# First-layer products of a maxout FFN as eleven block products instead of twelve, in the last two token groups

## The chip, the cores and the metric

The kernel runs on one core of one Trainium2 chip. The metric is the device time of one execution in microseconds (us), the median of several runs. Everything is float32.

## The reference

A DeltaNet attention (batch 4, 8 heads, 768 steps, head dimension 48) feeds a feed-forward block with a maximum of three linear layers (3072 tokens, width 384, hidden width 768):

```python
for t in range(S):
    kt, vt, bt = (k_n[:, :, t], v[:, :, t], beta[:, :, t, None])
    y[:, :, t] = np.einsum('bhd,bhde->bhe', q[:, :, t], state)
    v_old = np.einsum('bhde,bhd->bhe', state, kt)
    state = state + bt[:, :, :, None] * np.einsum('bhd,bhe->bhde', kt, vt - v_old)
...
h = np.maximum(np.maximum(x @ w1, x @ w2), x @ w3)
return (h @ w_out).astype(np.float32)
```

where `x` is `y` with the heads side by side: 3072 tokens of 384 numbers.

## The kernel before, in words

**Groups.** The sequence is cut into chunks of 64 steps. Two chunks of all four batches are a group of 512 tokens, and there are six groups, m = 0 to 5 (`GROUPS` = 6). For each group the kernel works out the recurrence (gram matrices, a triangular solve, state updates) and then the feed-forward block, `ffn(m)` (L1046). The two are interleaved: while TensorE does `ffn(m)`, the recurrence of group m+1 and the gram matrices and the solve of group m+2 are slipped in between its matmuls.

**Order.** The program is written in an order by hand (`manual_schedule`, L96): on every engine the instructions stand in the order in which the Python code issues them, and so do the DMAs on each queue. `ffn(m)` is a generator. The loop at L1320 takes it step by step; after step i it issues the small pieces that the table `LINKS` (L1210) names for i, then some columns of the solve (`some(solving, n)`, L1335). In the table a letter is a piece of work and a digit which chunk or unit it is for: k and q (the products of keys and queries with the state, L738, L747), z and j (two joining products of the triangular inverse, L694, L707), d (its turned copies on VectorE, L615), u (`new`, L753), s (state update, L771), y (L793), x, w and X (y goes to DRAM, comes back and is turned into the tokens `xt`, L833 to L866), g (gram matrices and their masks, L395), t (turned keys and queries, L375), and K, V, L, N (loads). Around the change the table is used with its last entries altered:

```python
LAST_LINKS = {**LINKS, 17: "", 19: "X1"}
```

**The first layer, `hidden` (L1050).** The second and third weights have had the first one subtracted (L868), and the first weight is multiplied into the output layer (L876 to L901), so from group 1 on a hidden tile is max(0, x·(w2−w1), x·(w3−w1)), and x·w1·w_out is added in the output layer. For each of six tiles of 128 hidden columns and each of the two weights, three matmuls (width 384 = 3 x 128) with 512 tokens moving fill one PSUM tile `p_h` (L1057), which ScalarE turns into `h` with a ReLU (L1067) or VectorE takes into the maximum (L1071). That makes twelve steps with 36 matmul instructions a group. `p_h` comes from `ps_ffn` (L80), two PSUM tiles of one bank in turn; the recurrence uses `ps_two` (L83), three tiles of two banks in turn.

**The output layer.** Groups 0 to 3 use plain matmuls (L1092). Groups 4 and 5 use `outputs` (L947), which already has seven products of 2x2 blocks in place of eight, with sums on VectorE (L989) and prepared weights `crossed` (`cross_weights`, L907, issued in `ffn(4)` at steps 8 and 9).

**The solve (L498).** For groups from 1 on, VectorE does 31 columns with two instructions each (L552, L556) on two tiles, `x_bl` and `y_bl`. `x_bl` comes from DRAM (L483), where the gram matrices `at` were put by 16 DMAs (L436). Ahead of the columns stand a square root on ScalarE (L261) and a dozen short VectorE instructions (L262 to L538). After the last column `y_bl` goes to DRAM (L577) and comes back as `ut` in eight DMAs (L586), which z needs. The solve of group 5 is done in `ffn(3)`; its last four `ut` loads are issued by `some(solving, 3)` after step 0 of `ffn(4)` (L1323).

Of the kernel before, what the change touches and what calls it, by code (L numbers as in the profile page):

```python
# [9 lines left out]
FP32 = mybir.dt.float32  # L10
# [4 lines left out]
ALU = mybir.AluOpType  # L15
# [3 lines left out]
BL = 32  # L19
HB = 16  # L20
# [3 lines left out]
def kernel(  # L24
# [31 lines left out]
    nc = tc.nc  # L56
# [5 lines left out]
    KT = DM // 128  # L62
    FT = DFF // 128
    NP = H // 2
    UNITS = NCH * 2
    GROUPS = UNITS // 4
    TOK = 512
# [4 lines left out]
    work = ctx.enter_context(tc.tile_pool(name="work", bufs=2))  # L72
# [7 lines left out]
    def ps_ffn(shape, name):  # L80
        return psum.tile(shape, FP32, name=name, tag="ffn", bufs=2)

    def ps_two(name):  # L83
        return psum.tile([128, 2, 512], FP32, name=name, tag="two", bufs=3)
# [3 lines left out]
    kmore = [const.tile([128, 2, H, DP], FP32, name=f"kmore{i}") for i in range(2)]  # L88
# [20 lines left out]
    def rows(bb):  # L109
        return slice(C * bb, C * (bb + 1))  # L110
# [25 lines left out]
    def load_v(c, queue=nc.sync):  # L136
        vts[c] = work.tile([128, 2, H, D], FP32, name="v_t", bufs=3)
        for bb in range(2):
            queue.dma_start(  # L139
                out=vts[c][rows(bb)].rearrange("p g h d -> p (g h) d"),  # L140
                in_=v[2 * bb : 2 * bb + 2, :, c * C : (c + 1) * C, :].rearrange(
                    "b h p d -> p (b h) d"
                ),
            )
# [36 lines left out]
    for bb in range(2):  # L181
        nc.gpsimd.affine_select(
            out=mask[rows(bb)], in_=mask[rows(bb)], pattern=[[1, C]], base=-1,
# [4 lines left out]
    t1 = [const.tile([128, 2, H, BL], FP32, name=f"t1{i}") for i in range(NU)]  # L188
# [5 lines left out]
    w_sb = [const.tile([128, KT, DFF], FP32, name=f"w{i}_sb") for i in range(3)]  # L194
# [112 lines left out]
    def square(name):  # L307
        return work.tile([128, H, C], FP32, name=name, tag="square", bufs=17)
# [39 lines left out]
    def load_blocks(n, queue=nc.gpsimd):  # L348
        c, g = divmod(n, 2)
        for i in range(2):  # L350
            if n % 4 == 2:
                t = kmore[i].rearrange("p a h d -> p (a h d)")[:, 0 : 2 * TURNED]
                t = t.rearrange("p (b x) -> p b x", b=2)
            else:
                t = work.tile(
                    [128, 2, TURNED], FP32, name="turned", tag="w_bits", bufs=5
                )
            turned[n, i] = t
            nc.gpsimd.memset(t[:, :, TURNED - 48 : TURNED], 0.0)  # L359
            for bb in range(2):  # L360
                for par in range(2):
                    for db in range(2):
                        p0, at = DP * par + 32 * db, 32 * (1 - db)
                        (queue, nc.gpsimd)[i].dma_start(  # L364
                            out=t[p0 : p0 + 32, bb, at : at + NP * 2 * D].rearrange(
                                "p (j x) -> p j x", j=NP
                            ),
                            in_=(k, q)[i][
                                2 * bb + g, :, c * C : (c + 1) * C, :
                            ].rearrange(  # L370
                                "(j two) (r tb) d -> two r j (tb d)", two=2, tb=2
                            )[par],
                        )
# [104 lines left out]
    def blocks(m, queue=nc.sync):  # L478
        if m == 1:
            xs[m] = in_wo(0)  # L480
        else:
            xs[m] = work.tile([128, 2, HB * BL + HB], FP32, name="x_bl", bufs=1)
        queue.dma_start(  # L483
            out=in_rows(xs[m]),
            in_=at_d[m].rearrange("c f b h j i -> (c f b h) j i"),
        )
# [232 lines left out]
    xts, rhss, qss, us, yts = {}, {}, {}, {}, {}  # L719
# [171 lines left out]
    def both_layers(t):  # L891
        p_m = ps_ffn([128, DM], "p_m")
        for f in range(FT):
            nc.tensor.matmul(  # L894
                p_m,
                w_sb[0][:, t, f * 128 : (f + 1) * 128],
                wo_sb[:, f],
                start=(f == 0),
                stop=(f == FT - 1),
            )  # L900
        nc.scalar.copy(w_sb[0][:, t, 0:DM], p_m)  # L901

    HALF = DM // 2
    PAIRS = FT // 2
    crossed = {}
# [41 lines left out]
    def outputs(m, hs):  # L947
# [95 lines left out]
        store(m5, 1, 1)  # L1043
        yield

    def ffn(m):  # L1046
        xt = xts[m]
        hs = {}

        def hidden(f, lo, w):  # L1050
            if f not in hs:
                hs[f] = square("h").rearrange("p h c -> p (h c)")
            h = hs[f][:, lo : lo + w]
            for i in range(m > 0, 3):
                p_h = ps_ffn([128, TOK], "p_h")[:, 0:w]
                for t in range(KT):
                    nc.tensor.matmul(  # L1057
                        p_h,
                        w_sb[i][:, t, f * 128 : (f + 1) * 128],
                        xt[:, t, lo : lo + w],  # L1060
                        start=(t == 0),
                        stop=(t == KT - 1),
                    )
                if i == 0:
                    nc.scalar.copy(h, p_h)
                elif m and i == 1:
                    nc.scalar.activation(  # L1067
                        out=h, in_=p_h, func=mybir.ActivationFunctionType.Relu
                    )
                else:  # L1070
                    nc.vector.tensor_tensor(out=h, in0=h, in1=p_h, op=ALU.max)  # L1071
                yield


        early = FT // 2 if m == 0 else 0
        for lo in (0, TOK // 2):
            for f in range(early):
                yield from hidden(f, lo, TOK // 2)
        for f in range(early, FT):
            yield from hidden(f, 0, TOK)  # L1080
        if m >= GROUPS - 2:
            yield from outputs(m, hs)
            return
        for i in range(4):
            cc, g = divmod(i, 2)
            p_o = ps_ffn([128, DM], "p_o")
            last = slice(i * 128, (i + 1) * 128)
            terms = [(hs[f][:, last], wo_sb[:, f]) for f in range(FT)]
            if m:
                terms += [(xt[:, t, last], w_sb[0][:, t, 0:DM]) for t in range(KT)]  # L1090
            for n, (stays, moves) in enumerate(terms):
                nc.tensor.matmul(  # L1092
                    p_o, stays, moves, start=(n == 0), stop=(n == len(terms) - 1)
                )
                if m and n == 4:
                    yield
            o_sb = work.tile([128, DM], FP32, name="o_sb")
            nc.scalar.copy(o_sb, p_o)  # L1098
            for bb in range(2):
                tok0 = (2 * bb + g) * S + (2 * m + cc) * C  # L1100
                nc.sync.dma_start(out=out[tok0 : tok0 + C, :], in_=o_sb[rows(bb)])
            yield
# [3 lines left out]
    def some(gen, n):  # L1106
        for _ in range(n):
            if next(gen, gen) is gen:
                break

    conv = weights()
    solving = solve(0)
# [71 lines left out]
    for _ in range(2):  # L1184
# [17 lines left out]
    solving = solve(1)  # L1202
# [33 lines left out]
        t=turn, K=load_k, L=lambda n: load_blocks(n, nc.sync),  # L1236
# [4 lines left out]
    def links(m, names):  # L1241
        for name in names.split():
            f, i = name[0], int(name[1])
            if f in RECURS and m < GROUPS:
                RECURS[f](2 * m + i)
            elif f in MADE and m + 1 < GROUPS:
                MADE[f](2 * (m + 1) + i)
            elif f in UNIT and m + 1 < GROUPS:
                UNIT[f](4 * (m + 1) + i)
            elif f == "N" and m + 2 < GROUPS:  # L1250
                load_blocks(4 * (m + 2) + i)
# [15 lines left out]
    for i, _ in enumerate(ffn(0)):  # L1267
# [17 lines left out]
        if i == 20:  # L1285
            solving = solve(2)
# [31 lines left out]
    UNIT.update(t=turn_blocks, K=lambda n: load_k(n, (nc.gpsimd, nc.gpsimd)))  # L1318
    MADE.update(V=lambda c: load_v(c, nc.gpsimd))
    for m in range(1, GROUPS):  # L1320
        for i, _ in enumerate(ffn(m)):
            if i == 0:
                some(solving, 3)  # L1323
            if m == 1 and i in (2, 5, 8):
                both_layers(i // 3)
            if m == GROUPS - 2 and i in (8, 9):
                cross_weights(i - 8)
            if m + 2 < GROUPS:
                if i == 6:
                    blocks(m + 2)  # L1330
                if i == 8:
                    solving = solve(m + 2)
            links(m + 1, (LAST_LINKS if m == GROUPS - 2 else LINKS).get(i, ""))
            if i > 7:
                some(solving, 3 if i > 8 else 1)  # L1335
# [29 lines left out]
```

## Time and profile before

| | |
|---|---|
| median of three runs | 514.99 us (511.83 to 518.12) |
| the profiled execution's own time | 514.26 us |
| its span, from the first to the last instruction | 512.3 us |
| VectorE, ScalarE, GpSimd busy | 324.2 us (63%), 163.7 us (32%), 192.3 us (38%) |
| `ffn(4)`, first layer, with recurrence pieces | 388.6 to 432.2 us |
| `ffn(4)`, output layer | 432.2 to 455.4 us |
| `ffn(5)`, first layer | 455.4 to 486.3 us |
| `ffn(5)`, output layer and stores | 486.3 to 512.3 us |

A line of the timeline reads: start in us, duration in us, engine, line of the code, operation, what is written and read, shape, count, and in brackets how long the engine had been idle and what ended that. PE is TensorE (PEld its weight loads), DVE VectorE, ACT ScalarE, POOL GpSimd, SPq the DMA queue of SyncE. A table of windows gives for each stretch its length, then the busy time and the number of instructions of each engine, the TensorE clock that was granted (1.00 is full speed), the share of DMA time and GB/s. A float32 matmul instruction appears as two records on PE, two passes: the first layer of group 5 has 36 instructions and 72 records.

### The profile page before, as it was taken

The numbers are of one execution on the slowest core, as the hardware profiler recorded it, in microseconds if no ns is written. First come the engines' busy times: TensorE is split into PE (matmuls) and PEld (weight loads), VectorE is DVE, ScalarE is ACT, GpSimd is POOL, SyncE is SP. The second block draws the span as 40 slices with busy tenths as digits, with TensorE's granted clock in tenths as the row PEclk, the third lists the DMA queues.
The fourth block names the chain that finished last, engine by engine and source line by source line (L and its number), as shares of the span: only waits on it lengthen the run. The fifth ranks groups of instructions, "written<-read, shape, count | busy, mean of one in ns | idle before, by whom it ended". The sixth has DMA issues, their size and how long they took to land.

```text
span 512.3 us, 18314 instructions
## 1 busy us (share of the span) xinstructions
PE 492.6 (96%) x7956; PEld 322.2 (63%) x7956; DVE 324.2 (63%) x735; ACT 163.7 (32%) x302; POOL 192.3 (38%) x317
## 2 busy tenths in 40 slices
PE   7778989999999999999999999999999999999996
PEld 6667778755565565665555565555655556974496
DVE  5897799868996430899553987635897244521142
ACT  5586664984422232200242101341101412101110
POOL 7444372783491925770575780503130000000000
PEclk9765999999999999999999999999999999999999
DMA  8938879874055926463775454823333202220002
GB/s 110 196 67 217 192 146 157 194 212 85 3 149 143 169 48 125 106 142 80 151 128 129 120 138 100 167 34 94 82 95 98 44 3 64 61 63 0 1 15 47
DMA packets 106303, 53.47 MB, mean 104 GB/s; under 512 B 89712, under 2 KB 99984, under 8 KB 106224
## 3 DMA queue, kind: packets, MB, share of 16 engines
q1 hardware_dynamic: 94640, 31.55, 30.9%
q0 software_dynamic: 9472, 20.37, 16.9%
q8 instruction: 62, 1.02, 0.9%
q10 hardware_dynamic: 2112, 0.39, 0.5%
q14 instruction: 17, 0.14, 0.1%
HBM read 39.17 MB, written 13.11 MB: 102 GB/s over the span
## 4 chain that ended last, share of the span: by engine, by line
PE 70%; DVE 15%; DMA 7%; issue 3%; ACT 2%; SPq 1%; POOL 1%; DVEq 0%; POOLq 0%; ACTq 0%
PE p_h L1057 31%; PE p_o L1092 13%; PE p_o L960 5%; DVE tmp L552 4%; PE p_g L406 3%; DVE y_bl L556 2%; PE p_m L894 2%; PE p_u L759 2%; DMA qall<-in_q_dram 2%; PE p_s L782 2%; PE p_k L731 1%; PE p_j L714 1%; PE p_y L801 1%; DMA x_bl<-at_d 1%; DMA y_x<-y 1%
## 5 line engine op out<-in xcount | busy, mean ns | idle before, releaser
L1057 PE MATMUL p_h<-xt,w_sb 128*128 128x512 f32 (+1 forms) x522 | 218.9, 564 | 0.7 <-ACT xt L827 0.6
L1057 PEld LDWEIGHTS p_h<-xt,w_sb 128*128 128x128 f32 x522 | 96.0, 193 | 85.7 <-issue 78.9
L1071 DVE TENSOR_TENSOR h<-h,p_h 128x512 f32<-128x512 f32 (+1 forms) x48 | 29.6, 616 | 86.5 <-PE p_h L1057 85.8
L1092 PE MATMUL p_o<-wo_sb,h 128*128 128x384 f32 x192 | 65.3, 490 | 0.0
L552 DVE TENSOR_TENSOR tmp<-x_bl,y_bl 128x31 f32<-128x31 f32 (+20 forms) x139 | 51.4, 369 | 4.1
L556 DVE TENSOR_TENSOR y_bl<-y_bl,tmp 128x31 f32<-128x31 f32 (+20 forms) x139 | 48.5, 349 | 4.8
L1092 PEld LDWEIGHTS p_o<-wo_sb,h 128*128 128x128 f32 x192 | 35.7, 190 | 23.2
L1067 ACT ACTIVATE h<-p_h 128x512 f32<-128x512 f32 x30 | 17.9, 597 | 98.4 <-PE p_h L1057 84.7
L364 POOL DMA_DIRECT2D turned<-in_q_dram x72 | 39.1, 551 | 6.7 <-POOL turned L359 2.5
L1098 ACT COPY o_sb<-p_o 128x384 f32<-128x384 f32 x16 | 7.7, 478 | 85.9 <-PE p_o L1092 79.8
L254 POOL TENSOR_TENSOR w_sb<-mant,up 128x384 int32<-128x384 int32 x18 | 18.8, 1046 | 39.4 <-DVE mant L250 38.7
L406 PEld LDWEIGHTS p_g<-kqt 48*64 48x64 f32 x1216 | 24.1, 138 | 9.4 <-issue 5.7
L406 PE MATMUL p_g<-kqt 48*64 48x64 f32 (+1 forms) x1216 | 27.5, 238 | 1.1 <-ACT kqt L335 0.8
L120 POOL DMA_DIRECT2D kpad<-in_k_dram x32 | 21.8, 690 | 14.0 <-issue 12.7
L789 DVE TENSOR_TENSOR st<-st,p_s 48x768 f32<-48x768 f32 (+1 forms) x18 | 17.1, 950 | 15.4 <-PE p_s L782 15.2
L1092 PE MATMUL p_o<-w_sb,xt 128*128 128x384 f32 x72 | 25.2, 486 | 0.0
L139 POOL DMA_DIRECT2D v_t<-in_v_dram x14 | 11.6, 830 | 35.1 <-PE p_u L759 35.1
L390 DVE TENSOR_TENSOR pt<-p_g,mask 128x512 f32<-128x512 f32 x20 | 13.8, 689 | 16.3 <-PE p_g L406 16.3
L287 POOL TENSOR_TENSOR v_t<-v_t,nrm 128x768 f32<-128x768 f32 x12 | 17.9, 1492 | 9.0 <-DVE nrm L281 8.9
L359 POOL MEMSET turned<- 128x96 f32 x18 | 3.3, 191 | 46.7 <-DVE kqt L380 46.7
L759 PEld LDWEIGHTS p_u<-v_t,ut 64*64 64x64 f32 x768 | 13.4, 142 | 10.1 <-issue 8.2
L1092 PEld LDWEIGHTS p_o<-w_sb,xt 128*128 128x128 f32 x72 | 13.7, 190 | 9.5
(171 smaller groups left out, 732.4 us busy)
## 6 DMA issues: line engine op xcount, KB each, us to landing
out_dram<-o_sb SPq DMA_DIRECT2D x40, 96.0 KB
w_bits<-in_moe_w_dram SPq DMA_DIRECT2D x9, 384.0 KB
w_bits<-in_moe_w_dram POOLq DMA_DIRECT2D x9, 384.0 KB, 5.3
turned<-in_q_dram POOLq DMA_DIRECT2D x72, 48.0 KB, 2.8
kpad<-in_k_dram POOLq DMA_DIRECT2D x32, 96.0 KB, 5.5
y_x<-y SPq DMA_DIRECT2D x16, 192.0 KB
qall<-y_x SPq DMA_DIRECT2D x32, 96.0 KB
v_t<-in_v_dram POOLq DMA_DIRECT2D x14, 192.0 KB, 5.0
```

Of the source, the lines that this page charges most:

```text
L120: queues[bb].dma_start(out=dst[rows(bb ^ g), :, 0:D], in_=src[2 * bb + g, :, c * C : (c + 1) * C, :].rearrange("h p d -> p h d"),)
L254: nc.gpsimd.tensor_tensor(out=dst.bitcast(I32), in0=mant_v.bitcast(I32), in1=up_v, op=ALU.add)
L287: nc.gpsimd.tensor_tensor(out=vts[c], in0=vts[c], in1=nrm[:, :, :, None].to_broadcast([128, 2, H, D]), op=ALU.mult,)
L364: (queue, nc.gpsimd)[i].dma_start(out=t[p0 : p0 + 32, bb, at : at + NP * 2 * D].rearrange("p (j x) -> p j x", j=NP), in_=(k, q)[i][2 * bb ...
L406: nc.tensor.matmul(p_g[rows(bb ^ (g * i)), par, c0 : c0 + C * (1 + whole)], kq[:, 0], kq if whole else kq[:, i],)
L552: nc.vector.tensor_tensor(out=t_v, in0=row.to_broadcast(t_v.shape), in1=column.to_broadcast(t_v.shape), op=ALU.mult,)
L556: nc.vector.tensor_tensor(out=rest, in0=rest, in1=t_v, op=ALU.subtract)
L759: nc.tensor.matmul(p_v[rows(bb ^ g), g, i], ut[c % NU][rows(bb), g, h], rhs[rows(bb), g, h],)
L960: nc.tensor.matmul(to[:, g], a[j][:, 128 * g : 128 * (g + 1)], b[j], start=(start and g == j == 0), stop=(stop and g == 1 and j == PAIRS - 1),
L1057: nc.tensor.matmul(p_h, w_sb[i][:, t, f * 128 : (f + 1) * 128], xt[:, t, lo : lo + w], start=(t == 0), stop=(t == KT - 1),)
L1071: nc.vector.tensor_tensor(out=h, in0=h, in1=p_h, op=ALU.max)
L1092: nc.tensor.matmul(p_o, stays, moves, start=(n == 0), stop=(n == len(terms) - 1))
```

## The change

In `ffn(4)` and `ffn(5)` the calls of `hidden` are replaced by `crossed_hidden`. The hidden width is cut into two halves of three tiles, the tokens into two halves of 256, and the width 384 into three parts of 128. For each of three pairs of tiles and each of the two weights (a "unit", six a group) the product of the first two parts is made with seven block products, and the third part with four plain ones: eleven matmul instructions of 256 moving tokens (twelve of this size before). They fill eight PSUM tiles in turn, called bank 0 to bank 7 here: even ones from `ps_two`, odd ones from `ps_ffn`, under names of their own (`p_c`, `p_e`). ScalarE copies four of them (products m1, m7, m5, m6) to SBUF; four sums of these (`plus`) are made by GpSimd in `ffn(4)` and by VectorE in `ffn(5)`; VectorE adds them to the other four banks and, for the second weight, takes the maximum. Four differences of the tokens (s1 to s4) are made by VectorE first. The products are kept in `x_bl` and `y_bl` in turn, s1 to s4 in one `kmore` tile. `cross_hidden(i)` makes four combinations of each weight's blocks with VectorE, in `ffn(3)` at steps 5 and 6. `some(solving, 3)` is called once more ahead of `ffn(4)`.

```diff
+    def cross_hidden(i):
+        n = PAIRS * 128
+        w = w_sb[i]
+        b11, b12 = w[:, 0, 0:n], w[:, 0, n : 2 * n]
+        b21, b22 = w[:, 1, 0:n], w[:, 1, n : 2 * n]
+        t = [
+            work.tile([128, 2, n], FP32, name="crossed", tag="w_bits", bufs=5)
+            for _ in range(2)
+        ]
+        t1, t2, t3, t4 = (t[n // 2][:, n % 2] for n in range(4))
+        for to, a, b in ((t3, b22, b12), (t1, b12, b11), (t2, b22, t1), (t4, b21, t2)):
+            nc.vector.tensor_tensor(out=to, in0=a, in1=b, op=ALU.subtract)
+        thirds[i] = dict(
+            b11=b11, b21=b21, b22=b22, t1=t1, t2=t2, t3=t3, t4=t4,
+            c1=w[:, 2, 0:n], c2=w[:, 2, n : 2 * n],
+        )
+
+    def crossed_hidden(m, hs):
+        xt, vec = xts[m], nc.vector.tensor_tensor
+        plus = vec if m == GROUPS - 1 else nc.gpsimd.tensor_tensor
+        lo, hi = slice(0, 256), slice(256, 512)
+        a11, a12, a13 = (xt[:, t, lo] for t in range(KT))
+        a21, a22, a23 = (xt[:, t, hi] for t in range(KT))
+        spare = [t.rearrange("p a h d -> p (a h d)") for t in kmore]
+        s1, s2, s3, s4 = (spare[0][:, 256 * n : 256 * (n + 1)] for n in range(4))
+        parts = [
+            work.tile([128, 2, HB * BL + HB], FP32, name=name, bufs=1).rearrange(
+                "p s r -> p (s r)"
+            )
+            for name in ("x_bl", "y_bl")
+        ]
+        vec(out=s3, in0=a11, in1=a21, op=ALU.subtract)
+        vec(out=s1, in0=a21, in1=a22, op=ALU.add)
+        vec(out=s2, in0=s1, in1=a11, op=ALU.subtract)
+        vec(out=s4, in0=a12, in1=s2, op=ALU.subtract)
+        for j in range(FT):
+            hs[j] = square("h").rearrange("p h c -> p (h c)")
+        for unit in range(2 * PAIRS):
+            j, i = divmod(unit, 2)
...
+            top, bottom = hs[j], hs[j + PAIRS]
+            held = parts[unit % 2]
+            m1, m5, m6, m7 = (held[:, 256 * n : 256 * (n + 1)] for n in range(4))
+            c11 = spare[1][:, 256 * (unit // 2 % 2) :][:, 0:256]
...
+            def result(h, base, p, spare=None):
+                to = h if i == 0 else base if spare is None else spare
+                vec(out=to, in0=base, in1=p, op=ALU.add)
+                if i:
+                    nc.vector.scalar_tensor_tensor(
+                        out=h, in0=h, scalar=0.0, in1=to, op0=ALU.max, op1=ALU.max
+                    )
+
+            def bank(n):
+                return (ps_ffn([128, TOK], "p_e") if n % 2 else ps_two("p_c")[:, 0])[
+                    :, 0:256
+                ]
+
+            p = bank(0)
+            times(p, ("b11", a11))
+            nc.scalar.copy(m1, p)
+            p = bank(1)
+            times(p, ("b21", a12), ("c1", a13))
+            result(top[:, lo], m1, p, c11)
+            p = bank(2)
+            times(p, ("t3", s3))
+            nc.scalar.copy(m7, p)
+            p = bank(3)
+            times(p, ("t1", s1))
+            nc.scalar.copy(m5, p)
+            yield
+            p = bank(4)
+            times(p, ("t2", s2))
+            nc.scalar.copy(m6, p)
+            plus(out=m6, in0=m6, in1=m1, op=ALU.add)
+            plus(out=m1, in0=m6, in1=m5, op=ALU.add)
+            plus(out=m7, in0=m7, in1=m6, op=ALU.add)
+            plus(out=m5, in0=m5, in1=m7, op=ALU.add)
+            p = bank(5)
+            times(p, ("c2", a13), ("b22", s4))
+            result(bottom[:, lo], m1, p)
+            p = bank(6)
+            times(p, ("t4", a22), ("c1", a23))
+            result(top[:, hi], m7, p)
+            p = bank(7)
+            times(p, ("c2", a23))
+            result(bottom[:, hi], m5, p)
+            yield
...
+        if m >= GROUPS - 2:
+            yield from crossed_hidden(m, hs)
+            early = FT
         for f in range(early, FT):
             yield from hidden(f, 0, TOK)
...
     for m in range(1, GROUPS):
+        if m == GROUPS - 2:
+            some(solving, 3)
         for i, _ in enumerate(ffn(m)):
...
+            if m == GROUPS - 3 and i in (5, 6):
+                cross_hidden(i - 4)
```

More of the change, by code (lines that the diff above doesn't have):

```diff
@@ L1044, in outputs @@
         yield
+    thirds = {}
+    def cross_hidden(i):
[14 more added lines that the diff above has]
+        )
@@ new lines, in crossed_hidden, with times @@
+    def crossed_hidden(m, hs):
[20 more added lines that the diff above has]
+            j, i = divmod(unit, 2)
+            w = {
+                name: t[:, 128 * j : 128 * (j + 1)]
+                for name, t in thirds[1 + i].items()
+            }
+            top, bottom = hs[j], hs[j + PAIRS]
+            held = parts[unit % 2]
+            m1, m5, m6, m7 = (held[:, 256 * n : 256 * (n + 1)] for n in range(4))
+            c11 = spare[1][:, 256 * (unit // 2 % 2) :][:, 0:256]
+            def times(to, *terms):
+                for n, (stays, moves) in enumerate(terms):
+                    nc.tensor.matmul(
+                        to, w[stays], moves, start=(n == 0), stop=(n == len(terms) - 1)
+                    )
[5 more added lines that the diff above has]
+                        out=h, in0=h, scalar=0.0, in1=to, op0=ALU.max, op1=ALU.max
+                    )
+            def bank(n):
[32 more added lines that the diff above has]
+            yield
```

## The prediction

> **What bounds the kernel now.** I read the page's totals first, then the windows of the last two groups, then the timeline at the places where the change puts work. The totals name TensorE:
>
> ```profile
> PE 492.6 (96%) x7956; PEld 322.2 (63%) x7956; DVE 324.2 (63%) x735; ACT 163.7 (32%) x302; POOL 192.3 (38%) x317
> ```
>
> The windows say that this holds in the stages concerned. Rows: first layer of group 4 with recurrence, first layer of group 5.
>
> ```profile
> 388.60:432.20 43.60, 43.34 (x842) 23.61 (x841) 18.24 (x39) 11.11 (x18) 0.00 (x0) 1.00 0.19 43
> 455.40:486.30 30.90, 30.90 (x74) 13.69 (x73) 3.98 (x6) 3.58 (x6) 0.00 (x0) 1.00 0.06 15
> ```
>
> TensorE is busy throughout at full clock, the others have room, so matmul time saved here would shorten the run, if nobody makes TensorE wait. Two places are tight. First, the start of group 4 (timeline):
>
> ```profile
> 388.64 2.76 PE L1057 MATMUL p_h<-xt,w_sb 128*128 128x512 f32 x6
> ...
> 392.39 0.21 DVE L556 TENSOR_TENSOR y_bl<-y_bl,tmp 128x31 f32<-128x31 f32 x1
> ```
>
> TensorE starts group 4 at 388.64, while VectorE is in the last columns of the solve until 392.60. Today nothing of `p_h` depends on that. Second, the start of that solve:
>
> ```profile
> 353.15 0.26 ACT L261 ACTIVATE root_bl<-x_bl 128x32 f32<-128x32 f32 x1 [1.37 <-DMA x_bl<-at_d]
> ...
> 354.02 0.17 DVE L262 TENSOR_SCALAR nt_bl<-root_bl 128x32 f32<-128x32 f32 x1
> ...
> 358.73 0.68 DVE L1071 TENSOR_TENSOR h<-h,p_h 128x512 f32<-128x512 f32 x1
> ...
> 359.47 0.30 PEld L1057 LDWEIGHTS p_h<-xt,w_sb 128*128 128x128 f32 x2 [0.22 <-DVE h L1071]
> ```
>
> The solve waits for its DMA, the maximum L1071 stands behind the solve's short instructions, and TensorE already waits 0.22 us for L1071. Slack from the DMA to TensorE is only about 0.6 us (353.41 to 354.02).
>
> **What the skill says.** (1) The Trainium skill, SBUF — State Buffer, "Who interferes with whom": a VectorE instruction with two SBUF inputs and a GpSimd one that reads SBUF exclude each other for a whole instruction. The trace agrees: L552 of 60 elements, 0.22 us elsewhere, takes 0.90 beside a GpSimd sum.
>
> ```profile
> 120.64 1.03 POOL L254 TENSOR_TENSOR wo_sb<-mant,up 128x384 int32<-128x384 int32 x1 [0.36 <-DVE tmp L552]
> 120.84 0.90 DVE L552 TENSOR_TENSOR tmp<-x_bl,y_bl 128x60 f32<-128x60 f32 x1
> ```
>
> (2) TensorE: Matmul & The Clock Gate, "What's actually happening": an idle stretch of about a 3.4 us window halves TensorE's clock, a busy one restores it. In this trace even gaps of 2.12 us (ended 16.12) and 2.75 us (ended 29.29) were followed by half clock, for 7 and 23 us:
>
> ```profile
> 14.00:16.00 2.00, 0.00 (x0) 0.00 (x0) 1.53 (x7) 1.67 (x4) 0.04 (x1) 1.00 1.37 186
> 16.00:18.00 2.00, 1.88 (x36) 1.58 (x40) 1.55 (x6) 0.58 (x1) 1.18 (x2) 0.51 0.83 108
> ```
>
> After 54 us no gap exceeds 1.3 us and the clock stays at 1.00.
>
> **The change part by part.**
>
> *Matmuls removed.* 72 records of 512 took 30.90 us: 0.429 each. Six records of 256 in group 0 spread over 1.46 us with 0.38 for the last: (1.46−0.38)/5 = 0.216. A group needs 66 instructions, 132 records: 28.5 against 30.9 us. Gain 2.4 a group, **−4.8**. One product is 0.432 us, a unit (11) 4.75.
>
> *cross_hidden in ffn(3).* Eight subtractions of 384, 0.56 each (L989, same shape): 2.2 us at each of two steps. The second four fall into VectorE's wait of 5.98 us before 347.75: nothing; without that cover 2.2. The first four stand ahead of the masks L390 (340.10 and 341.07), whose bank ScalarE then copies to `at`; the copies end at 343.9 instead of 342.4. Behind them on SP's queue: eight L436 DMAs, then `x_bl`. So `x_bl` lands 1.6 to 1.85 late, L262 starts 1.0 to 1.3 late, and L1071 and TensorE with it. VectorE's later idle 1.62 us before L803 doesn't help, since TensorE itself is late. Between 0 (if the later load runs faster) and 1.3; I take **+1.2**.
>
> *some(solving, 3) moved.* Four `ut` DMAs (0.5 us each on SP) stand where they stood in SP's queue, right behind their neighbours: 0.
>
> *Start of group 4.* In the new order bank 2 needs s3, which VectorE makes only behind the solve's last column. TensorE does three products, to 388.64+1.30 = 389.94, then waits for 392.60+0.42 (a 256-wide L989) = 393.02. Queued behind it: everything on TensorE, the k and q products too. **+3.1**. ScalarE's m1 copy waits for `x_bl` to be free as well, at the same moment.
>
> *Clock.* That gap is longer than both gaps that were followed by half clock. Then two products, k and q (2.0 us at full clock) and part of the unit run at half speed, some 6 us until dense work restores it: half of that is lost. From 0 (clock stays) to 4.4; I take **+3.0**.
>
> *GpSimd's sums, group 4.* No 256-wide one is in the trace. Price of the skill, GPSIMD Engine Reference, "Elementwise — side-by-side cycle accounting": about 156 ns and 2.6 cycles an element at 1.2 GHz; estimate for 384: 0.99 (trace: L254 1.00); for 256: 0.71. Scaling L287 (1.49 for 768) gives 0.50; at worst 1.0. I take 0.72. GpSimd is otherwise idle there (0.00 in the window) except one L287. The chain from the end of bank 4: 0.2 to start the copy and 0.36 for it (L1065), four sums 2.9, VectorE's last addition 0.41 (L1071 of 256), 3.9 in all. TensorE wants that bank again (bank 3 of the next unit) after nine products, 3.9. No slack: whatever holds m6's copy shows. Ahead of it on ScalarE stand a qs copy (0.80) twice, z and j copies (2.4 each), a u copy (0.80); on VectorE at step 8 L914, L918, L789 and L803 (4.4 us); and the maxima have two SBUF inputs and are locked out by GpSimd's sums (up to 0.7). Unit by unit I get stalls of 0.3, 0 (z's matmuls cover), 0.65, 0.95, 0.3 = 2.2; and 0.65 at j, whose turned copies wait behind the unit's sums. **+2.9**, from 1.3 (sum of 0.5) to 7.4 (1.0). Half clock hides the first stall: **−0.3**. Back comes the wait of z today for `ut` (z took 1.92 against 1.35 in ffn(3)), since TensorE now arrives later: **−0.5**.
>
> *VectorE's sums, group 5.* Two units take 20 VectorE instructions of 0.34 to 0.46 us (six independent L989 take 2.09; dependent pairs of L552 and L556 step by 0.46): 8 us against 9.5 of TensorE. It fits, but after a unit with maxima the last addition comes 4.15 us after bank 4's end where TensorE wants the bank at 3.9: 0.26 twice, and 0.4 at the handover to `p_o`. **+1.0**, from 0.3 to 3.
>
> *The rest.* 24 ScalarE copies of 0.36 a group: hidden in group 5. Hidden tiles reserved early and the output layer's order: no change.
>
> Sum: −4.8+1.2+3.1+3.0+2.9−0.3−0.5+1.0 = **+5.6**. Against the profiled execution's own 514.26 (span 512.3 and 2.0 around it) that is 519.9. The median is 0.73 above that execution: 520.6 on its scale.
>
> **The rivals.** *A, the sum above*: 520.6, chance 0.55, its own range 518 to 524.
> *B, the clock holds* through the gap at group 4's start: +5.6−3.0+0.3 = +2.9, 517.9, so not slower by what can be measured. For it: a gap of 3.1 us straddling two windows may idle neither fully; against: both gaps over 2 us in the trace. It decides from a gap of about 2 us on, or not at all below 3.4. Chance 0.18.
> *C, handoffs are cheap*: GpSimd sums of 0.5, the late load catches up, clock holds: −4.8+3.1+1.3−0.5+0.5 = −0.4, 514.6. For it: L287's rate; against: L254's. Chance 0.06.
> *D, GpSimd becomes the bound*: at 1.0 us a sum four boundaries cost 1.1 more each: 520.6+4.5 = 525.1. For it: L254's 1.00 for 384 and the lock; against: the price above. Chance 0.18.
> *E, the matmul gain arrives whole*, with s3 made early somehow: 510.2; the order of the built program speaks against. 0.03.
>
> **How the numbers follow.** A measurement here can tell about 1% (5.1 us) from no change; slower by more begins at 520.1. A lies above with 0.6 of its 0.55 (0.33), D wholly (0.18): slower 0.51. Faster is E, 0.03. The rest, 0.46, within 1%. For 8 in 10 I leave out C, E and the top of D: 516 to 526, A's own range being 518 to 524.
>
> **What would show it.** TensorE idle for about 3 us at 390 to 394 waiting for VectorE's s3, with a granted clock of 0.5 in the next windows; L262 starting about 1 us later; records of 256 every 0.216; GpSimd sums near 0.72 and TensorE waiting for `h` or `y_bl` additions at bank 3 in group 4; group 5's first layer near 29.5 us. The prediction is wrong if s3 is there before TensorE, if GpSimd's sums take 0.5 or 1.0, or if group 5 runs over 31 us because VectorE can't keep up.

## The result, and the profile after

The changed kernel took 520.24 us (median of 18 runs, 516.62 to 525.60), the kernel before 513.62 us on the same chip (18 runs): ratio 1.0126, 95% interval 1.0104 to 1.0147, about 6.6 us slower. The same kernel in a later comparison gave 1.0092 (1.0063 to 1.0122). The predicted 520.6 us was right as a number; the working behind it was right only in part.

The profiled execution after took 521.26 us, with a span of 519.4. The page's totals:

```profile
PE 492.7 (95%) x8076; PEld 345.0 (66%) x8076; DVE 359.5 (69%) x835; ACT 173.3 (33%) x338; POOL 209.5 (40%) x341
```

TensorE's busy time is what it was (492.6) though its products should take 4.8 us less, and the span is 7 us longer: the saving has become waiting, part of it inside records that count as busy. The windows of the same two stages (length, then busy time and count of PE, PEld, DVE, ACT, POOL, then granted clock, DMA share, GB/s) show where:

```profile
393.50:439.60 46.10, 42.94 (x901) 34.18 (x899) 26.68 (x60) 16.17 (x36) 18.23 (x25) 1.00 0.18 39
462.46:493.01 30.55, 30.16 (x134) 24.23 (x133) 23.11 (x61) 8.93 (x24) 0.00 (x0) 1.00 0.06 13
```

In group 4 TensorE was busy for all but 0.3 us of its stage before; now it idles over 3 us of 46.1. In group 5, whose 66 products should take 28.5 us, 0.4 us are idle; the rest of the loss is in records that are a tenth or two of a microsecond longer and count as busy.

One caution on comparing these two profiles. Up to the first `p_u` of `ffn(3)` (343.72 us before, 346.49 after) TensorE does the same in both programs, and from the first matmul of `ffn(3)` to it it takes 27.9 and 28.1 us, so these 2.8 us are chance: in nine of the profiles below the same point lies between 341.2 and 346.0, in the changed kernel's second one at 343.0. All stages are therefore counted from this mark, M. Two of the later profiles are of slow executions: the one with even distance in both groups was taken while the granted clock stayed at 0.95, so from it only waits are read, and the changed kernel's second one (523.25 us) fell to half clock twice behind M.

| stage, in us | before | after | difference |
|---|---|---|---|
| M to group 4's first matmul | 44.92 | 47.07 | +2.15 |
| group 4, first layer | 43.51 | 46.07 | +2.56 |
| group 4, output layer | 23.15 | 22.83 | −0.32 |
| group 5, first layer | 30.90 | 30.55 | −0.35 |
| the rest | 26.09 | 26.41 | +0.32 |
| M to the end | 168.57 | 172.93 | +4.36 |

The start of the solve in `ffn(3)`, timeline of after (L1071 and L1057 of before are L1175 and L1161 here):

```profile
345.31 1.18 ACT L423 COPY at<-p_g 128x512 f32<-128x512 f32 x2 [4.80 <-DVE pt L390]
...
358.64 0.26 ACT L261 ACTIVATE root_bl<-x_bl 128x32 f32<-128x32 f32 x1 [4.09 <-DMA x_bl<-at_d]
358.93 0.18 DVE L262 TENSOR_SCALAR nt_bl<-root_bl 128x32 f32<-128x32 f32 x1 [2.07 <-ACT root_bl L261]
...
364.39 1.12 PE L1161 MATMUL p_h<-xt,w_sb 128*128 128x512 f32 x2 [2.25 <-DVE h L1175]
```

The chain predicted is there link by link: ScalarE's copies wait for the masks, the square root starts 2.7 us later after M than before, VectorE waits for the square root, and TensorE 2.25 us for VectorE's maximum. The start of group 4:

```profile
393.99 1.03 PE L1102 MATMUL p_e<-xt,w_sb 128*128 128x256 f32 x4
395.63 0.67 PE L1102 MATMUL p_c<-kmore,crossed 128*128 128x256 f32 x2 [0.61 <-DVE kmore L1083]
...
396.66 1.15 PE L731 MATMUL p_k<-st,kqt 48*64 48x48 f32 x64
```

The predicted wait, for the predicted instruction (L1083 makes s3), but 0.61 us long and not 3.1; `p_k` takes its usual 1.15 us, so the clock held. Why it was short, the next lines show, first of before, then of after. In before VectorE's L552, 0.42 us elsewhere at this size, took 2.80 us while GpSimd ran L287:

```profile
374.31 2.80 DVE L552 TENSOR_TENSOR tmp<-x_bl,y_bl 128x252 f32<-128x252 f32 x1
375.33 1.49 POOL L287 TENSOR_TENSOR v_t<-v_t,nrm 128x768 f32<-128x768 f32 x1
```

```profile
379.23 0.42 DVE L552 TENSOR_TENSOR tmp<-x_bl,y_bl 128x252 f32<-128x252 f32 x1
...
418.03 1.47 POOL L287 TENSOR_TENSOR v_t<-v_t,nrm 128x768 f32<-128x768 f32 x1
```

This L287 is issued in `ffn(4)` (p1 at step 5). Before, nothing stood ahead of it on GpSimd, so it ran at once, in the middle of the solve. Now group 4's sums stand ahead of it, and it comes 40 us later. The solve gets 2.4 us back: though VectorE began it (L262) 2.1 us later after M, it ended at nearly the same distance (48.88 before, 48.67 after), while TensorE came 2.15 us later; so the wait shrank. Nobody meant this, and no step of the prediction saw it.

The handoffs of group 4, TensorE's timeline with the longer waits:

```profile
408.70 0.70 PE L1102 MATMUL p_c<-xt,w_sb 128*128 128x256 f32 x2 [0.64 <-DVE y_bl L1108]
...
417.09 1.13 PE L1102 MATMUL p_e<-xt,w_sb 128*128 128x256 f32 x4 [0.53 <-DVE h L1108]
425.96 0.70 PE L1102 MATMUL p_e<-kmore,crossed 128*128 128x256 f32 x2 [0.78 <-DVE y_bl L1108]
```

L1108 is VectorE's addition that empties a bank. GpSimd's sums take 0.72 to 0.73 us, all but one of them, as predicted (0.72).

### The profile page after: what moved, and what is told of

It is laid out like the page before. It is cut to its first block, busy times and chain, and to the rows that moved or that the text cites. A ratio compares the mean times of both kernels' runs of the same rounds, so it can differ in the third digit from the quotient of the medians.

```text
span 519.4 us, 18760 instructions
## 1 busy us (share of the span) xinstructions
PE 492.7 (95%) x8076; PEld 345.0 (66%) x8076; DVE 359.5 (69%) x835; ACT 173.3 (33%) x338; POOL 209.5 (40%) x341
## 4 chain that ended last, share of the span: by engine, by line
PE 66%; DVE 17%; issue 5%; DMA 5%; POOL 3%; ACT 2%; SPq 1%; DVEq 0%; POOLq 0%; ACTq 0%
PE p_h L1161 20%; PE p_o L1199 13%; PE p_o L960 8%; PE p_e L1102 4%; DVE tmp L552 3%; PE p_g L406 3%; PE p_c L1102 3%; DVE y_bl L556 2%; PE p_m L894 2%; DMA x_bl<-at_d 2%; PE p_u L759 2%; PE p_k L731 2%; DMA at_d<-at 2%; PE p_y L801 1%; PE p_t L329 1%
## 5 line engine op out<-in xcount | busy, mean ns | idle before, releaser
L1161 PE MATMUL p_h<-xt,w_sb 128*128 128x512 f32 (+1 forms) x378 | 154.6, 550 | 2.8 <-DVE h L1175 2.3
L1161 PEld LDWEIGHTS p_h<-xt,w_sb 128*128 128x128 f32 x378 | 69.1, 193 | 56.3 <-issue 47.5
L552 DVE TENSOR_TENSOR tmp<-x_bl,y_bl 128x31 f32<-128x31 f32 (+20 forms) x139 | 49.0, 352 | 4.1
L1175 DVE TENSOR_TENSOR h<-h,p_h 128x512 f32<-128x512 f32 (+1 forms) x36 | 21.3, 592 | 33.4 <-PE p_h L1161 31.9
L406 PEld LDWEIGHTS p_g<-kqt 48*64 48x64 f32 x1216 | 25.4, 147 | 9.1 <-issue 7.0
L406 PE MATMUL p_g<-kqt 48*64 48x64 f32 (+1 forms) x1216 | 28.5, 247 | 0.6 <-ACT kqt L335 0.6
L1102 PE MATMUL p_e<-xt,w_sb 128*128 128x256 f32 x96 | 27.4, 388 | 0.6 <-DVE h L1108 0.5
L789 DVE TENSOR_TENSOR st<-st,p_s 48x768 f32<-48x768 f32 (+1 forms) x18 | 17.1, 950 | 14.1 <-PE p_s L782 14.0
L1171 ACT ACTIVATE h<-p_h 128x512 f32<-128x512 f32 x18 | 10.7, 597 | 39.2 <-PE p_h L1161 33.1
L287 POOL TENSOR_TENSOR v_t<-v_t,nrm 128x768 f32<-128x768 f32 x12 | 17.9, 1492 | 11.2 <-DVE nrm L281 11.1
L1102 PEld LDWEIGHTS p_e<-xt,w_sb 128*128 128x128 f32 x96 | 17.5, 189 | 5.6 <-DVE h L1108 2.4
```

What stands on the lines that cost most here:

```text
L287: nc.gpsimd.tensor_tensor(out=vts[c], in0=vts[c], in1=nrm[:, :, :, None].to_broadcast([128, 2, H, D]), op=ALU.mult,)
L406: nc.tensor.matmul(p_g[rows(bb ^ (g * i)), par, c0 : c0 + C * (1 + whole)], kq[:, 0], kq if whole else kq[:, i],)
L552: nc.vector.tensor_tensor(out=t_v, in0=row.to_broadcast(t_v.shape), in1=column.to_broadcast(t_v.shape), op=ALU.mult,)
L1102: nc.tensor.matmul(to, w[stays], moves, start=(n == 0), stop=(n == len(terms) - 1))
L1161: nc.tensor.matmul(p_h, w_sb[i][:, t, f * 128 : (f + 1) * 128], xt[:, t, lo : lo + w], start=(t == 0), stop=(t == KT - 1),)
```

## The experiments

All were timed in the same way, each against the kernel before on its own chip. The question throughout was whether each recorded loss is real: the late solve in `ffn(3)`, the start gap of group 4 with the clock behind it, the handoffs. Against it stood that the program as a whole is slower, that single losses are absorbed, that GpSimd is the bound, and, after the first profile, that delay and gap replace each other. Each expectation says which of these its theories 1 and 2 are.

**Only the weights' subtractions.** The changed kernel without `crossed_hidden`: the kernel before with `cross_hidden` in `ffn(3)`, its results unused (both first layers stay with `hidden`), and the added `some(solving, 3)`:

```diff
-        if m >= GROUPS - 2:
-            yield from crossed_hidden(m, hs)
-            early = FT
```

> The kernel before plus only the eight VectorE subtractions of cross_hidden in ffn(3), whose results nobody reads. Theory 1 (the change's cost begins in ffn(3): the first four subtractions delay the masks, the at_d DMAs, the x_bl load and with it the solve's start and the maximum that TensorE waits for): slower by 2 to 2.7 us, the x_bl square root some 2.5 us later, everything before ffn(3) unmoved in the median. Theory 2 (the kernel after is late from the start, as its profile shows 2.7 us before its first changed instruction; an effect of the program as a whole): here the same 0 to 1 us.

Measured: 513.99 us, ratio 1.0013 (0.9991 to 1.0034). The time is theory 2's (0 to 1 us), not the 2 to 2.7 us of theory 1; the profile has theory 1's chain, smaller: the square root comes 1.8 us later after M, TensorE waits 1.37 us for the maximum in `ffn(3)` and starts group 4 1.3 us later, the size recorded; at the end 0.8 us are left. By itself this part costs nothing that can be measured.

**The subtractions behind the masks.** In the changed kernel `cross_hidden` is issued behind `links(...)` at the same steps:

```diff
-            if m == GROUPS - 3 and i in (5, 6):
-                cross_hidden(i - 4)
...
             links(m + 1, (LAST_LINKS if m == GROUPS - 2 else LINKS).get(i, ""))
+            if m == GROUPS - 3 and i in (5, 6):
+                cross_hidden(i - 4)
```

> The kernel after with cross_hidden issued behind the masks and the other recurrence pieces of its step instead of ahead of them. Theory 1: ffn(3) costs nothing any more and TensorE comes to group 4 two us earlier, but then waits 2.5 to 3.1 us there for the token difference s3 behind the solve's last column (0.6 us in the profile after): most of the gain is given back, 1 to 4 us over the kernel before if the clock holds. Sub-question of the recorded prediction: does that gap halve the granted clock (then 4 to 6 us over before)? Theory 2 (whole program): 6.6 us over before as the kernel after.

Measured: 517.65 us, ratio 1.0074 (1.0044 to 1.0104). M to group 4 takes 44.9 us, as before: the late `x_bl` came from the place ahead of the masks. But TensorE now waits 2.96 us for L1083 (387.56 to 390.52), and in this execution the clock fell behind it. Windows of this run:

```profile
387.46:390.87 3.41, 0.45 (x3) 0.34 (x3) 3.07 (x13) 0.37 (x1) 0.00 (x0) 1.00 0.25 58
390.87:394.29 3.42, 3.42 (x84) 2.70 (x86) 1.19 (x4) 0.74 (x2) 0.00 (x0) 0.50 0.65 161
394.29:397.70 3.41, 3.41 (x65) 2.96 (x58) 0.90 (x1) 1.17 (x2) 0.24 (x1) 0.50 0.60 94
397.70:401.11 3.41, 3.41 (x17) 2.94 (x16) 1.42 (x4) 0.38 (x1) 2.62 (x4) 1.00 0.37 58
```

6.8 us at half clock cost 3.4: that is the recorded "Clock" step, in place and size. L287 comes behind group 4's sums here too, and L552 takes 0.42 us, yet the solve ends no earlier than before (48.87 us after M): VectorE now waits for a DMA that L861 needs.

```profile
384.65 1.24 DVE L861 STREAM_TRANSPOSE xt<-qall 128x768 f32<-128x768 f32 x1 [2.26 <-DMA qall<-y_x]
```

So with a solve that starts in time, what L287 held up was free; only in a solve that starts late, as in the changed kernel, does L287's place count.

**Group 5 alone.** As the last one, with `crossed_hidden` only for `m >= GROUPS - 1`.

> Block products in group 5 alone, group 4 as before, cross_hidden behind the masks. Theory 1: ffn(3) and group 4 cost nothing, group 5 gains what it shows in the profile after, 0.8 us: 0.5 to 1.2 us faster than before. Theory 2: no gain, 0 to 3 us slower.

Measured: 513.58 us, ratio 1.0007 (0.9983 to 1.0031). The gain of theory 1 doesn't show in the time; in the profile M to the end is 0.8 us shorter. Group 5's first layer takes 30.56 us, as in the changed kernel: of 2.4 us that the products save, 2.05 are lost at banks, 0.5 of it at the handover to the output layer. So the slowdown belongs to group 4 and to the place of the subtractions.

**Group 4's sums on VectorE.** `plus = vec` for both groups.

> The kernel after with the four sums of each unit on VectorE in group 4 too. Theory 1 (the chain of four GpSimd sums of 0.72 us and its lock against VectorE's two-input maxima hold TensorE's banks in group 4): 1 to 2.5 us faster than the kernel after. Rival (VectorE has no room for them beside the recurrence, whose in-order pieces then hold the banks): as slow as the kernel after or up to 2 us slower.

Measured: 521.64 us, ratio 1.0136 (1.0078 to 1.0194), six runs. Group 4's first layer takes 47.57 us, without its start gap 44.6; in the run with the subtractions behind the masks, where GpSimd makes the sums, it takes 51.04, without gap and half clock (2.96 and 3.4) 44.7. So GpSimd isn't the bound, and it isn't to blame for the handoffs. With no GpSimd sums ahead of it, L287 is back at its old place, and the gap is back, here without a slow `p_k`:

```profile
392.19 0.67 PE L1102 MATMUL p_c<-kmore,crossed 128*128 128x256 f32 x2 [2.97 <-DVE kmore L1083]
...
393.22 1.15 PE L731 MATMUL p_k<-st,kqt 48*64 48x48 f32 x64
```

**The changed kernel again,** with no edit.

> The changed kernel once more, unchanged. Theory 1 (the delay of TensorE in ffn(3) and the gap at group 4's start are alternatives: what is lost in ffn(3) isn't lost again at group 4): the distance from the first p_u of ffn(3) to the first L960 of outputs(4) comes out near 93.1 us again, with either a late L262 and a gap under 1 us, or an early L262 and a gap of about 3 us. Theory 2 (each is lost by itself, and the first profile was a lucky one at group 4): about 95 to 96 us, a late L262 and a gap of 2.5 to 3 us together. Ratio 1.011 to 1.014 for both.

Measured: 518.23 us, ratio 1.0092 (1.0063 to 1.0122); its profiled execution took 523.25. M to the first L960: 98.5 us. Neither figure fits (93.1, or 95 to 96): a wait of 2.03 us in `ffn(3)` and one of 1.90 at group 4 were each followed by half clock.

```profile
360.68 4.54 PE L1161 MATMUL p_h<-xt,w_sb 128*128 128x512 f32 x6 [2.03 <-DVE h L1175]
...
394.90 0.67 PE L1102 MATMUL p_c<-kmore,crossed 128*128 128x256 f32 x2 [1.90 <-DVE kmore L1083]
395.41 1.00 PE L1102 MATMUL p_e<-kmore,crossed 128*128 128x256 f32 x2
396.34 1.96 PE L731 MATMUL p_k<-st,kqt 48*64 48x48 f32 x64
```

Six records of 512 take 2.84 us at full clock, here 4.54. The idea that delay and gap are alternatives falls: here both come, each with its clock. The gap was 1.90 and not 0.6, and the solve ended 51.43 us after M and not 48.67: VectorE waited 1.19 us for the DMA of `qall` ahead of L861, which SP's queue started 3.3 us later after M than in the first profile, behind the half clock in `ffn(3)`.

**L287 at its old place.** In the changed kernel p1's product is issued at the end of `ffn(3)`, ahead of group 4's sums:

```diff
+            if m == GROUPS - 3 and i == 17:
+                links(m + 1, "P1")
```

> The changed kernel with GpSimd's last product L287 issued at the last step of ffn(3), ahead of group 4's sums, where it ran in the kernel before. Theory 1 (in the kernel before that product held VectorE's L552 for 2.8 us, and the change moved it away by the order of GpSimd's queue, so that the solve ends earlier): the solve ends 2 to 2.5 us later against the first L262 than in the changed kernel, TensorE's wait for L1083 at group 4's start grows from 0.6 to 2.5 to 3 us, time 522 to 525 (ratio to the kernel before 1.016 to 1.022). Theory 2 (the product's place makes no difference to the end of the solve): gap 0.6, time as the changed kernel, 520 (1.012).

Measured: 524.08 us, ratio 1.0197 (1.0155 to 1.0239), six runs, as theory 1 said. The timeline has all of it:

```profile
376.39 2.80 DVE L552 TENSOR_TENSOR tmp<-x_bl,y_bl 128x252 f32<-128x252 f32 x1
377.41 1.49 POOL L287 TENSOR_TENSOR v_t<-v_t,nrm 128x768 f32<-128x768 f32 x1
...
395.19 1.19 PE L1102 MATMUL p_c<-kmore,crossed 128*128 128x256 f32 x2 [3.01 <-DVE kmore L1083]
...
397.16 1.96 PE L731 MATMUL p_k<-st,kqt 48*64 48x48 f32 x64
```

L552 is held for 2.80 us again, the gap is 3.01 us, and the clock is halved from 394.7 to 404.9. Of the 2.4 us by which the gap is longer than in the profile after, 1.5 come from the solve's later end (50.16 us after M); the other 0.9 come from TensorE, which waited less in `ffn(3)` (1.35 us) and came earlier. In this kernel a delay of TensorE by 1.25 us in `ffn(3)`, the gap of 3.01 and the clock stand one after another: they add up, as recorded. So the change was spared some 4 to 6 us (524.08 against 520.24 and 518.23) by an instruction that it pushed aside; the times are the evidence for this, the profiles for the way.

**Group 4's terms on GpSimd.** The subtractions behind the masks, and s1 to s4 of group 4 off VectorE:

```diff
-        vec(out=s3, in0=a11, in1=a21, op=ALU.subtract)
+        plus(out=s3, in0=a11, in1=a21, op=ALU.subtract)
```

and likewise s1, s2, s4.

> The changed kernel with the weights' subtractions behind the masks, and with group 4's s1 to s4 made by GpSimd instead of VectorE (L1083 to L1086 no longer stand behind the solve's last columns). Theory 1 (the start of group 4 lost about 3 us and sometimes the clock because s3 stood behind the solve): TensorE's gap at bank 2 is gone or under 1 us, a wait of 0.5 to 1.5 us for the first h of bank 1 or for m1's copy comes later at bank 4 or 5, no drop of the clock; time 513 to 515.5 (ratio 0.998 to 1.004, against 1.0074 with the terms on VectorE). Theory 2 (the solve holds m1's copy and h just as long, so the gap only moves to bank 4 or 5): a gap of 2 us or more there, time 516.5 to 518.

Measured: 516.41 us, ratio 1.0068 (1.0047 to 1.0088), above the 513 to 515.5 of theory 1 and just under theory 2's 516.5, whose gap at bank 4 or 5 isn't there. The trace shows theory 1's mechanism all the same: no loss in `ffn(3)`, no gap at the start, no drop of the clock.

```profile
390.55 0.59 PE L1102 MATMUL p_c<-kmore,crossed 128*128 128x256 f32 x2
...
391.50 1.15 PE L731 MATMUL p_k<-st,kqt 48*64 48x48 f32 x64
392.85 1.15 PE L731 MATMUL p_q<-st,kqt 48*64 48x48 f32 x64 [0.19 <-ACT x_bl L1121]
```

Still group 4's first layer takes 45.6 us against 43.5, with the start clean: the handoffs alone cost more than the products save. Adding up the steps from each record's start to the next: 66 products of 0.432 us are 28.5; they occupy 33.0. Before, 36 instructions (31.0) occupied 32.2. Of the 4.5 us, 2.0 are three waits for L1108 and L789; the other 2.5 are two dozen losses of 0.07 to 0.2 us. Half of these come where TensorE changes to a recurrence piece and back, as before (1.2 us); the other half, at a dozen further banks, is new.

**Eight banks in group 5.** Group 5 alone; banks 2 and 3 from `ps_ffn`, the other six as halves of two-bank tiles:

```diff
-                return (ps_ffn([128, TOK], "p_e") if n % 2 else ps_two("p_c")[:, 0])[
-                    :, 0:256
-                ]
+                if n in (2, 3):
+                    return ps_ffn([128, TOK], "p_e")[:, 0:256]
+                if n % 2 == 0:
+                    pairs[n // 2] = ps_two("p_c")
+                return pairs[n // 2][:, n % 2, 0:256]
```

> Products of eleven in group 5 alone (group 4 as in the kernel before), and the eight banks of a unit all distinct: banks 2 and 3 from the pool of one-bank tiles, the others as halves of two-bank tiles. Theory 1 (group 5 keeps only 0.8 of its 2.4 us because TensorE waits for a bank whose sum VectorE has not finished): the first layer of group 5 takes 28.5 to 29.2 us and the time is 512.0 to 512.6 (ratio 0.996 to 0.998; with the banks as changed it was 1.0007). Theory 2 (VectorE's sums bind whatever the banks, or two-bank tiles wait for their later half): as with the banks as changed, 513.2 to 514.5.

Measured: 525.94 us, ratio 1.0256 (1.0206 to 1.0305), six runs, far outside both theories.

```profile
481.40 0.37 ACT L1138 COPY y_bl<-p_c 128x256 f32<-128x256 f32 x1
481.83 0.70 PE L1102 MATMUL p_c<-xt,w_sb 128*128 128x256 f32 x2 [0.46 <-ACT y_bl L1138]
...
484.67 1.13 PE L1102 MATMUL p_c<-xt,w_sb 128*128 128x256 f32 x4 [0.85 <-DVE y_bl L1108]
486.26 1.13 PE L1102 MATMUL p_c<-xt,w_sb 128*128 128x256 f32 x4 [0.46 <-ACT x_bl L1125]
```

(Line numbers are this kernel's own.) TensorE waits before each second half until ScalarE or VectorE has read the first half of the same two-bank tile: the wait that theory 2 names, but 18 times and 10 us in all. There are more banks, but each of these handoffs is now on the path. As a test of theory 1 it says nothing, since it brought a wait of its own.

**Even distance in group 5.** Group 5 alone, with the five buffers in even turn, so that a bank is wanted again after five and not, for the odd ones, after four:

```diff
-                return (ps_ffn([128, TOK], "p_e") if n % 2 else ps_two("p_c")[:, 0])[
+                one = (8 * unit + n) % 5 in (0, 3)
+                return (ps_ffn([128, TOK], "p_e") if one else ps_two("p_c")[:, 0])[
```

> Products of eleven in group 5 alone, with the banks at an even distance of five. Theory 1: group 5's excess over its bare products of 2.05 us (0.08 to 0.2 at each of a dozen banks, 0.5 at the end) falls to about 1.2, time 512.4 to 513.2 (ratio 0.998 to 0.9995; with the banks as changed 1.0007). Theory 2 (the late ones are VectorE's sums, which gain no time by it): 1.9 or more, ratio 1.000 to 1.002.

Measured: 511.26 us against 513.48, ratio 0.9965 (0.9946 to 0.9983): faster than both kernels. First layer of group 5:

```profile
452.90:481.40 28.50, 28.50 (x133) 24.93 (x132) 22.67 (x59) 8.96 (x24) 0.00 (x0) 1.00 0.06 15
```

It runs from 452.87 to 481.40: 28.53 us, the bare 66 x 0.432. Theory 1 is borne out, and beyond its figure: VectorE's sums were in time, they only held the wrong bank.

**Even distance in both groups.** As the run with the terms on GpSimd, with the same turn of banks.

> As the run with group 4's terms on GpSimd, but the eight banks of a unit taken from the five buffers at an even distance (one-bank, two, two, one-bank, two and so on) instead of every odd one from the two one-bank buffers. Theory 1 (the handoffs of group 4 show because a sum's bank is wanted again after four banks): the waits of 0.64, 0.52 and 0.78 us for L1108 in group 4 shrink to under 0.3 each, first layer of group 4 at 43.5 to 44.3 us instead of 45.6, time 514.0 to 515.2 (ratio 1.001 to 1.004). Theory 2 (what is waited for is the sums themselves, at any distance of the banks): 516 to 517, as with the terms on GpSimd (1.0068).

Measured: 516.64 us, ratio 1.0083 (1.0051 to 1.0115): nothing gained in group 4. TensorE's waits there:

```profile
412.89 1.61 PE L1102 MATMUL p_c<-xt,w_sb 128*128 128x256 f32 x6 [0.56 <-DVE y_bl L1108]
...
417.25 0.75 PE L714 MATMUL p_j<-z,t 32*32 32x32 f32 x64 [1.12 <-DVE h L1108]
...
433.98 0.68 PE L1102 MATMUL p_c<-xt,w_sb 128*128 128x256 f32 x2 [1.82 <-DVE st L789]
```

The wait for `h` at a product (0.52) is gone, but j waits 1.12 us for a bank in its place, and a product 1.82 us for L789, which reads the recurrence's `p_s`. The likely reason, which no run separates: the recurrence takes the same two-bank buffers in between, so the turn is even only on paper, and each bank is wanted sooner by someone. Whether buffers of its own would bring group 4 its gain wasn't tried.

## Why the prediction was right in time, and where it failed

- *Matmuls removed (−4.8):* right. Records of 256 step by 0.216 us; group 5 ran in exactly 28.53 us once nothing held it.
- *cross_hidden (+1.2):* right in chain and cause (the subtractions behind the masks take it away). TensorE's wait was 1.13, 1.35 and 1.37 us in three of the kernels above; in the changed kernel's own profiles 2.25 and 2.03, as `x_bl` landed later still (the square root 12.15 and 11.93 us after M, against 11.03 to 11.27 in the three). There the term was short by about 1. A small misreading: the 0.22 us that TensorE "already waits" are its weight load's; the products themselves had no gap there.
- *Start of group 4 (+3.1):* right in mechanism; 2.96, 2.97 and 3.01 us in three of the kernels above. In the changed kernel itself 0.61 and 1.90. The prediction moved TensorE and the solve by the same 1.2 us, so that the gap stayed; measured, TensorE came 2.15 us later and the solve ended 0.2 earlier. The step that failed is the sentence on GpSimd: "GpSimd is otherwise idle there (0.00 in the window) except one L287". It counts L287 as load on GpSimd and didn't ask where the new sums push it in GpSimd's queue, nor what it had been holding up. The run with L287 at its old place shows it: 2.80 us for L552, 50.16 for the solve's end, 3.01 for the gap, 524.08 us.
- *Clock (+3.0):* in the profile after, 0. Elsewhere the half clock behind group 4's gap lasted 6.8 or 10.2 us and so cost 3.4 or 5.1, and behind 2.97 us it didn't come. It depends on where the gap falls in time (below), and so differs by execution; the prediction made it a step of the sum, and had the right reason against it in rival B, a gap that straddles two windows.
- *GpSimd's sums (0.72 each):* right to the digit. The estimates of 0.99 and 0.71 hold some 0.16 us beside the 2.6 cycles an element; the trace bears that part out, with 1.00 for 384 elements and 0.72 for 256. *Handoffs of group 4 (+2.9, and −0.5 for z's wait):* too small. In the profile after the units' products lose 3.35 us more than before without the start gap (predicted 2.2), j 0.81 (predicted 0.65), and z gives nothing back: its wait for `ut` goes, but a wait of 0.64 us for `y_bl` stands behind it, where the prediction had "0 (z's matmuls cover)". Together 4.2 against 2.4. What was left out are the losses of 0.07 to 0.2 us at a dozen further banks, some 1.3 us.
- *VectorE's sums in group 5 (+1.0):* measured 2.05 over the bare products: 1.5 in such losses and 0.5 at the handover to `p_o`. All of it went when no bank came round after four.

In the profile after the terms from M are: −4.8 for the products, about +2.2 in `ffn(3)`, +0.75 for the start, +4.2 and +2.05 for handoffs: +4.4, beside +4.36 in the table. The recorded sum was +5.6. So gap and clock (5.8 with the stall that they were to hide) came out 5.1 too high, the rest 3.9 too low; the number was right by cancellation. That is luck. The difference of the medians is larger (6.6, and 4.7 us in the second comparison, 513.53 to 518.23). A part is the clock: the mean granted clock on record for each execution (twice what it lacks of 1, times the span) makes it some 36 us of half clock in the median of the 18, against 31 in the profiled one, and 32 to 34 in the medians of the kernel before in the later comparisons. An estimate from this is 1 to 2 us of the 6.6; the rest isn't shown. Rival D (GpSimd the bound) is refuted by its 0.72 us and by the run with VectorE's sums; rival E's gain exists, in group 5 alone, with another turn of banks.

## What to carry to other kernels

When an engine gets new work, look at what already stood in its queue behind that place: an instruction that used to run early because nothing was ahead of it moves too, and with it whatever it held up or was held up by. What was held up may have been free before, because something else was late anyway; check what comes next on the path. In group 5 the saving on the bound engine came through only once every result buffer came round later than its reader was done: count the distance in buffers, for each kind of buffer and with everyone who shares it, before counting the arithmetic. And stages that add small waits at each handoff should be charged for all of them, not only for the long ones.

## What the hardware showed that was not expected

- The granted clock doesn't follow from the length of a gap alone. Half clock followed waits of 1.90, 2.03, 2.96 and 3.01 us; full clock stayed after 2.25 and 2.97. The Trainium skill, TensorE: Matmul & The Clock Gate, "What's actually happening", speaks of a free-running window of about 3.4 us; all six gaps are shorter. The traces show what decides here. Between the first and the last change of the clock, every stretch at one clock is a multiple of 3.41 us long (3.41, 6.83, 10.24 and so on), in all profiles: the changes lie on a grid. In the run with the subtractions behind the masks the wait of 2.96 us fell into one step of it, with TensorE busy for 0.45 of 3.41 us (the first window there). In the run with VectorE's sums the wait of 2.97 us straddled two steps, each busy for over half:

```profile
387.35:390.76 3.41, 1.87 (x8) 1.14 (x6) 3.07 (x12) 0.48 (x1) 0.00 (x0) 1.00 0.25 56
390.76:394.17 3.41, 1.98 (x68) 1.62 (x72) 2.78 (x9) 1.12 (x3) 0.00 (x0) 1.00 0.39 78
394.17:397.59 3.42, 3.42 (x91) 3.11 (x83) 2.03 (x4) 1.07 (x2) 0.00 (x0) 1.00 0.49 120
```

The same count gives 0.93, 1.38 and 1.51 us busy ahead of the half clock behind 3.01, 2.03 and 1.90 us, and at least 1.86 in the two steps of the 2.25 us that left it full. So in these stages a step busy for 1.51 us of 3.41 or less halved the clock of the next, and one busy for 1.86 or more did not. It isn't a rule for the first 66 us of the runs: there steps busy for two thirds were followed by half clock too.

- A VectorE instruction held by a GpSimd one lost more than that one's length: 0.42 became 2.80 us beside an L287 of 1.49 us, in all seven profiles in which L287 runs at that place in the solve and in none of the other five. Why it is longer isn't shown.
- A product into one half of a two-bank PSUM tile waited each time for the reader of the other half, 0.46 us behind ScalarE's copy, 0.5 or 0.85 behind VectorE's addition. Whether the chip needs this wait, or only the program's own synchronization makes it, isn't shown.
